# Copies of three weight sets move from GpSimd to SyncE, and the opening's steps get a new order

## The chip, the cores and the metric

The kernel runs on one NeuronCore of a Trainium2 chip. The core has five engines with an instruction stream each: TensorE (PE in the profile, with PEld for its weight loads), VectorE (DVE), ScalarE (ACT), GpSimd (POOL) and SyncE (SP), which here does nothing but issue DMAs. Sixteen DMA engines move the data. Each engine works through its own stream in program order; an instruction that waits holds everything behind it on that engine. The metric is the time of one execution on the device in microseconds.

## What is computed

The input x has 2048 rows of 576 floats. Its layer norm feeds two branches, and both are added to x:

```python
x = A_x
xn = _layernorm(x, axis=-1)
return x + _A_ref(xn, A_wqkv, A_wo) + _B_ref(xn, B_w1, B_w2)
```

Branch A is attention with 32 heads of 18 features. Each position looks at 8 keys, at distances 0, 2, ... 14 backwards; `wqkv` is 576 x 1728 and `wo` is 576 x 576. Branch B is `relu(xn @ w1) @ w2` with `w1` 576 x 4608 and `w2` 4608 x 576. All is float32, and the matrix products have to be that exact.

## The kernel before

**Precision and tiling.** Each float32 operand of a matmul is split into a high part (a copy to the matmul's float type, on ScalarE) and a low part (the rest, a subtraction on VectorE, in the opening sometimes on GpSimd), both by `hi_lo`. A product is then three matmuls: high by high, high by low and low by high. The rows of x are handled in two phases (`ph`) of 1024 rows, each in two halves (`h`) of 512, each in two blocks (`j`) of 256. The first products, of xn with `w1` and `wqkv`, use a Strassen-like scheme with seven products P1 to P7 in a step (`pstep`); a step covers one weight set and one half of the rows.

**Weight sets.** The columns of `w1` and `wqkv` are cut into sets of 256. A set of kind F is a piece of `w1` (with the matching rows of `w2`), one of kind Q a piece of `wqkv`. In phase 0 the order is F0, Q0, Q1, F1, Q2, F2, Q3 and so on; these are sets 0, 1, 2, 3, 4, 5, 6. Two buffers `wset` hold two sets at a time. For set s, `set_make` issues six loads on SyncE, from a copy of the set in DRAM that lies in the order in which it is read (`W1C`, `W2C`, `WQC`: w1c, w2c, wqc in the profile). One of the six goes to the tile `ts` and the others to slots of `wset`. VectorE then forms the Strassen combinations, and ScalarE and VectorE form the high and low parts.

**The copies.** They are made in the kernel itself by DMAs within DRAM. In the regular course each is cut into pieces by `w1_keep`, `w2_keep` and `wq_keep`, four row blocks with a DMA for each column segment. `kept_part` (lines 478 to 484) issues a piece on GpSimd's queue. Ahead of each piece it puts a one-element copy into the tile `spare` that reads the latest tile of hidden values, `LATEST[-1]`, so that the pieces are paced by the progress of the work. Sets from number 5 on get such pieces through the plan of the main loop. Sets 2, 3 and 4 get them in the opening, by the steps K2, K3 and K4 (`keep_set`, line 1251).

**The opening.** Sets 0 and 1 are read straight from the inputs and used without Strassen, in steps written out by hand in `OPEN`, line 34. The letters are:

- `T`i: block i of 128 normalised rows is transposed by PE and stored in parts; this also gives out the normalising of block i+2
- `F`hjf: 14 matmuls of set 0 (`classic`), for half h, block j and column group f; the result goes through relu into a hidden tile `hb`
- `Q`hjf: 14 matmuls of set 1; VectorE transposes the result into a staging buffer `stg` (`q_out`), and when both blocks j of a pair (h, f) are in, SyncE stores the buffer to DRAM (`qd`)
- `B` and `O`: hidden tiles times `w2`, summed into the banks `po`; O steps are six matmuls each and are named O, then half, block, column group, row half. After the last one of a bank ScalarE copies the sum away and seeds the bank anew.
- `S`h: the Strassen sums of the rows of half h. The raw rows of the last two blocks lie in the tile `ts` until S1 has read them.
- `K`s: the DRAM copy of set s
- `M`: `set_make(2)`, the loads and conversions of set 2

Then the main loop runs steps t = 4, 5, ... (two for each set). At the first product of t = 4 it calls `set_make(3)`, at t = 6 `set_make(4)`. Set 5's copies come at t = 5 and 6.

**What sets the order.** PE's instructions are given out in the order of the steps. A planner in the kernel (`Order`) keeps a modelled clock for each engine and gives out the operations of ScalarE and VectorE in between: of those that are ready by its model, the one with the earliest due time. `dve(fn, n, after, slack)` hands it an operation with a modelled duration of n/960 + 0.068 us; `send` does so for a DMA on SyncE and `keep` for one on GpSimd. The planner decides the order only. At run time each instruction waits for the data that it needs.

Of the kernel before, what the change touches and what calls it, by code (L numbers as in the profile page):

```python
# [16 lines left out]
P = 128  # L17
NPH = 2
NI = 8
TBN = 256  # L20
# [11 lines left out]
WARM = 38  # L32
PADS = (16, 16, 32, 32)
OPEN = """
B0 T2 B1 T3 Q000 F010 T4 Q011 O0100 F011 T5 Q010 O0101 S0 T6 F101
F100 O0111 T7 S1 Q001 K2 O0110 Q100 O1001 O1000 F110 O1011 F111 K3 O1010 M2
O1101 O1111 K4 Q110 Q101 O1100 O1110 Q111
""".split()

S2, S4, S3, S1 = range(4)  # L40
T1, B11, T2, B21, T3, B22, T4, RR = range(8)
# [21 lines left out]
class Order:  # L63
# [94 lines left out]
    def dve(self, fn, n, after, slack, lag=0.0):  # L158
        op = Op(DVE, n / 960.0 + 0.068, fn, after, self.now() + slack, lag)
        self.wait[DVE].append(op)  # L160
        return op
# [6 lines left out]
    def send(self, fn, kb, after=(), margin=0.0):  # L168

        after = [a for a in after if a is not None]  # L170
        self.force(after)
        start = max([self.clk[SP], self.now() - 0.5] + [a.end for a in after])
        fn()
        op = Op(SP, 0.45, None, (), 0.0)
        self.clk[SP] = start + 0.45
        rate, tail = (250.0, 2.2) if start < 16 else (185.0, 1.2)
        self.dma = max(self.dma, start + 0.3, 1.0) + kb / rate
        op.end = max(start + 2.1, self.dma + tail) + margin
        return op
# [28 lines left out]
def tile_body(ctx: ExitStack, tc: tile.TileContext, x, wqkv, wo, w1, w2, out):  # L208
    nc = tc.nc
    S, D = x.shape  # L210
    F = w1.shape[1]
# [22 lines left out]
    def wide(s):  # L234
        return QW[SETS[s][2]] if SETS[s][1] == "Q" else P
# [9 lines left out]
    SEGS = [[] for _ in range(NQ)]  # L245
    y = 0
    for part, u, c0, c1 in FEATS:
        while c0 < c1:
            q, off = y // (2 * P), y % (2 * P)
            cnt = min(c1 - c0, 2 * P - off)  # L250
# [26 lines left out]
    act, dve, send, pe = o_.act, o_.dve, o_.send, o_.pe  # L277
# [190 lines left out]
    W1C = [dram.tile([D, 2 * P], F32, name=f"w1c{n}") for n in range(NP)]  # L468
    W2C = [dram.tile([2 * P, D], F32, name=f"w2c{n}") for n in range(NP)]
    WQC = [dram.tile([D, 2 * QW[q]], F32, name=f"wqc{q}") for q in range(NQ)]  # L470
# [3 lines left out]
    kept = {}  # L474
# [132 lines left out]
    T6 = 6 * 0.1135  # L607
# [3 lines left out]
    def stub():  # L611
        return Op(SP, 0.0, None, (), 0.0)
# [28 lines left out]
    def q_out(t, j, f, src, after, slack):  # L641
        s, h = t // 2, t % 2
        ph, _, q = SETS[s]
        wd = wide(s)
        if (t, f) not in STGOF:
            b = STGN[0] % NST
            STGN[0] += 1
            STGOF[t, f] = b, [], [], STGFREE[b], stub()
            STGFREE[b] = [STGOF[t, f][4]]
            QOUT.setdefault((ph, q), []).append(STGOF[t, f][4])  # L650
        b, got, ops, before, done = STGOF[t, f]

        def turn():
            if not got:
                got.append(stp[b].tile([P, 2, TBN], F32, name=f"stg{b}"))
            nc.vector.transpose(got[0][0:wd, j], src[0:wd])

        op = dve(turn, TBN, [*after, *before], slack)
        ops.append(op)

        def out_():
            if len(ops) < 2 or any(z.end is None for z in ops):
                return
            z = got[0]
            for a in range(wd // 32):
                dst = QD[ph, q][4 * h : 4 * h + 4, :, f * wd + 32 * a : f * wd + 32 * (a + 1)]
                e = send(
                    lambda: nc.sync.dma_start(
                        dst.rearrange("i (b r) c -> r (i b) c", r=32),
                        z[32 * a : 32 * (a + 1)].rearrange("r j (z c) -> r (j z) c", c=32),  # L670
                    ), 80, ops,
                )
            done.end = e.end

        op.post = out_
        return [op]

    def evict(t, j, f, src, after, slack):
        s, h = t // 2, t % 2
        ph, kind, n = SETS[s]  # L680
        if kind == "F":
            return h_parts((2 * (ph * NP + n) + h, j, f), src, after, slack)
        return q_out(t, j, f, src, after, slack)
# [566 lines left out]

    def keep_set(s):
        ph, kind, n = SETS[s]
        for f in [w1_keep, w2_keep] if kind == "F" else [wq_keep]:
            for z in range(4):
                f(n, z)
    for z in range(8):
        at_f(7 + z // 4, 3 * (z % 4) + 2, wo_keep, z)
    for z in range(4):
# [224 lines left out]
    def opening(step):  # L1483
        kind, z = step[0], [int(c) for c in step[1:]]
        if kind == "B":
            o_both(*z)
        elif kind == "T":
            turn_one(*z)
        elif kind == "Q":
            classic(2 * SQ0 + z[0], z[1], z[2], next_bank())  # L1490
        elif kind == "F":
            classic(z[0], z[1], z[2], next_bank())
        elif kind == "O":
            o_step(*z)
        elif kind == "K":
            keep_set(*z)
        elif kind == "S":
            h = z[0]
            SX[h] = s_forms(h, 30 + 2 * h)
            if h:  # L1500
                ts_free[0] = SX[1]
                SNF[5], SNF[2] = list(SX[0]), list(SX[1])
                VDONE[:] = SX[0]
                OFREE[1] = list(SX[1])
        elif kind == "M":
            set_make(2, True)
            for f in range(2):
                if SF[1] == 2:
                    w2_make(1, f)
# [10 lines left out]
    for t in range(4, 2 * NS):  # L1520
        ph, kind, n = SETS[t // 2]
# [48 lines left out]
```

## Time and profile before

| What | us |
|---|---|
| median of 3 runs | 1121.61 |
| lowest and highest | 1120.93 and 1122.43 |
| the profiled execution's own time | 1122.29 |
| its span, first to last instruction | 1120.5 |
| mean granted clock of TensorE | 0.996 of full |

The page gives each engine's busy time as a share of the span. A line of a timeline has the start, the duration, the engine, the line and the operation; several instructions in a row of one kind are drawn together with their count. `SPq` is SyncE's queue of DMA issues. A duration there runs from the first issue of the row to the end of the last, with what SyncE waited between them. The chain of waits goes back from the last instruction to what released it, step by step.

### The profile page before, as it was taken

The numbers are of one execution on the slowest core, as the hardware profiler recorded it, in microseconds if no ns is written. First come the engines' busy times: TensorE is split into PE (matmuls) and PEld (weight loads), VectorE is DVE, ScalarE is ACT, GpSimd is POOL, SyncE is SP. The second block draws the span as 40 slices with busy tenths as digits, with TensorE's granted clock in tenths as the row PEclk, the third lists the DMA queues.
The fourth block names the chain that finished last, engine by engine and source line by source line (L and its number), as shares of the span: only waits on it lengthen the run. The fifth ranks groups of instructions, "written<-read, shape, count | busy, mean of one in ns | idle before, by whom it ended". The sixth has DMA issues, their size and how long they took to land.

```text
span 1120.5 us, 24120 instructions
## 1 busy us (share of the span) xinstructions
PE 1103.9 (99%) x9047; PEld 1100.9 (98%) x9047; DVE 910.5 (81%) x1749; ACT 757.3 (68%) x1561; POOL 247.6 (22%) x506
## 2 busy tenths in 40 slices
PE   9979999999999999999999999999999999999998
PEld 8979999999999999999999999999999999999998
DVE  7657999999998989954785698989998998997440
ACT  7646666666678677686794666667677776767774
POOL 4744365243443533700110000000000000000000
PEclk9989999999999999999999999999999999999999
DMA  5489487857655463363364844564625315224212
GB/s 153 94 189 240 118 210 181 192 148 200 180 152 160 122 185 91 85 173 94 92 192 83 193 99 89 135 130 86 149 91 119 105 47 140 75 55 86 79 48 86
DMA packets 326502, 144.16 MB, mean 129 GB/s; under 512 B 209648, under 2 KB 306608, under 8 KB 325104
## 3 DMA queue, kind: packets, MB, share of 16 engines
q1 hardware_dynamic: 315408, 113.40, 41.1%
q0 software_dynamic: 10816, 28.92, 9.2%
q8 instruction: 71, 1.16, 0.5%
q14 instruction: 47, 0.39, 0.1%
q10 hardware_dynamic: 160, 0.30, 0.1%
HBM read 118.42 MB, written 50.66 MB: 151 GB/s over the span
## 4 chain that ended last, share of the span: by engine, by line
PE 92%; DMA 2%; ACT 2%; POOL 2%; DVE 1%; issue 1%; SPq 0%; DVEq 0%; ACTq 0%; POOLq 0%
PE po L341 44%; PE bk L341 28%; PE pm L341 13%; PE bkA L341 8%; DMA wset<-w1c 1%; POOL wqc L482 1%; POOL spare L481 1%; DMA wset<-wqc 0%; DMA x<-in_x 0%; ACT wset L335 0%; DVE bst L376 0%; ACT xs L335 0%; ACT po L335 0%; SPq L528 0%; PE pm L411 0%
## 5 line engine op out<-in xcount | busy, mean ns | idle before, releaser
L341 PE MATMUL po<-w2t,hb 128*128 128x256 f32 (+1 forms) x3456 | 503.7, 292 | 1.1 <-ACT po L335 1.1
L341 PEld LDWEIGHTS po<-w2t,hb 128*128 128x128 f32 x3456 | 463.1, 187 | 1.6 <-ACT po L335 1.5
L335 ACT ACTIVATE x<-po 128x576 f32<-128x576 f32 x286 | 186.3, 652 | 227.9 <-PE po L341 227.3
L341 PE MATMUL bk<-xs,wset 128*128 128x256 f32 (+1 forms) x1584 | 224.3, 278 | 0.8 <-ACT sn L335 0.8
L341 PEld LDWEIGHTS bk<-xs,wset 128*128 128x128 f32 (+1 forms) x1584 | 202.8, 187 | 1.1 <-ACT sn L335 1.0
L335 ACT ACTIVATE po<-x 128x576 f32<-128x576 f32 x286 | 187.1, 654 | 6.1
L481 POOL COPY spare<-hb 1x1 f32<-1x1 f32 x228 | 106.9, 469 | 201.2 <-ACT hb L335 201.2
L341 PE MATMUL bk<-xa,wset 128*128 128x256 f32 (+1 forms) x888 | 125.7, 279 | 3.8 <-ACT wset L335 3.7
L341 PEld LDWEIGHTS bk<-xa,wset 128*128 128x128 f32 (+1 forms) x888 | 114.1, 188 | 4.3 <-ACT wset L335 3.8
L341 PE MATMUL pm<-xs,wset 128*128 128x256 f32 (+1 forms) x720 | 103.5, 280 | 3.7 <-ACT sn L335 3.2
L1113 POOL TENSOR_SCALAR_AFFINE_SELECT lg<-lg 1x512 f32<-1x512 f32 x8 | 9.6, 1206 | 416.8 <-DVE lg L1110 416.8
L338 DVE TENSOR_TENSOR sn<-bk,sn 128x256 f32<-128x256 f32 (+1 forms) x132 | 55.3, 420 | 52.0 <-ACT hb L335 25.2
L341 PEld LDWEIGHTS pm<-xs,wset 128*128 128x128 f32 (+1 forms) x720 | 93.2, 189 | 4.2 <-ACT sn L335 3.4
L1107 DVE TENSOR_TENSOR pr<-qo,kk 128x1152 f32<-128x1152 f32 x64 | 85.5, 1347 | 5.4 <-DMA qo<-qd 3.7
L341 PE MATMUL bkA<-xa,wset 128*128 128x256 f32 (+1 forms) x624 | 88.2, 278 | 0.5 <-ACT bkA L335 0.5
L1110 DVE TENSOR_REDUCE lg<-pr 128x64 f32<-128x1152 f32 x64 | 85.4, 1340 | 0.2
L1139 DVE TENSOR_TENSOR pr<-lg,v 128x1152 f32<-128x1152 f32 x64 | 85.4, 1351 | 0.2
L341 PEld LDWEIGHTS bkA<-xa,wset 128*128 128x128 f32 (+1 forms) x624 | 81.5, 187 | 0.7 <-ACT bkA L335 0.7
L335 ACT ACTIVATE hb<-sn 128x256 fp32r<-128x256 f32 x140 | 57.4, 414 | 35.7 <-DVE sn L338 34.3
L341 PE MATMUL bk<-xr,wset 128*128 128x256 f32 (+1 forms) x412 | 80.4, 276 | 0.0
L338 DVE TENSOR_TENSOR wset<-ts,wset 128x512 fp32r<-128x512 f32 (+2 forms) x98 | 65.2, 666 | 10.5 <-ACT wset L335 10.1
L1146 DVE TENSOR_TENSOR pr<-pr 128x288 f32<-128x288 f32 (+1 forms) x128 | 71.6, 600 | 0.0
(159 smaller groups left out, 1574.0 us busy)
## 6 DMA issues: line engine op xcount, KB each, us to landing
w2t<-w2c SPq DMA_DIRECT2D x70, 288.0 KB, 3.4
qd<-stg SPq DMA_DIRECT2D x216, 64.0 KB, 2.1
wset<-w1c SPq DMA_DIRECT2D x105, 128.0 KB, 2.9
w1c<-in_w POOLq DMA_DIRECT2D x72, 144.0 KB, 3.4
w2c<-in_w POOLq DMA_DIRECT2D x72, 144.0 KB, 3.3
out<-x SPq DMA_DIRECT2D x16, 288.0 KB, 2.1
ts<-w1c SPq DMA_DIRECT2D x35, 128.0 KB, 2.8
wset<-w1c SPq DMA_DIRECT2D x70, 64.0 KB, 2.3
```

What stands on the lines that cost most here:

```text
L335: nc.scalar.activation(o, i, func)
L338: nc.vector.tensor_tensor(o, a, b, op=op)
L341: nc.tensor.matmul(o, l, r, start=start, stop=stop, skip_group_check=True)
L481: nc.gpsimd.tensor_copy(spare[0:1], f32(LATEST[-1])[0:1, 0:1])
L482: nc.gpsimd.dma_start(dst, src)
L1107: nc.vector.tensor_tensor(pr[i], q, window(k, i), op=ALU.mult)
L1110: nc.vector.tensor_reduce(s["lg"][:, i], pr.pop(i).rearrange(heads, d=Dh), axis=AX.X, op=ALU.add)
L1113: nc.gpsimd.affine_select(out=z, in_=z, pattern=[[1, NI], [1, W], [0, HG]], compare_op=ALU.is_ge, fill=-1e9 / scale, base=1 - W, channel_m ...
L1139: nc.vector.tensor_tensor(pr[i].rearrange(heads, d=Dh), e, window(VV[u % 2], i).rearrange(heads, d=Dh), op=ALU.mult)
L1146: nc.vector.tensor_tensor(o, z[:, 0:n], z[:, n : 2 * n], op=ALU.add)
```

## The change

Three things change. `OPEN` gets a new order, with the same steps. K2 stands after the first Q step and not behind Q001, K3 comes right after Q001, and K4 follows M2. `keep_set` no longer calls the paced pieces of GpSimd: it issues whole copies on SyncE, one for each column segment of a Q set (four for set 2, three for set 4) and two for the F set 3, with no element copy ahead of them. The planned duration of the transpose in `q_out` grows by 25 elements, 26 ns in the planner's model.

```diff
 OPEN = """
-B0 T2 B1 T3 Q000 F010 T4 Q011 O0100 F011 T5 Q010 O0101 S0 T6 F101
-F100 O0111 T7 S1 Q001 K2 O0110 Q100 O1001 O1000 F110 O1011 F111 K3 O1010 M2
-O1101 O1111 K4 Q110 Q101 O1100 O1110 Q111
+B0 T2 B1 T3 Q000 K2 F010 F011 T4 Q011 O0101 T5 O0100 S0 O0110 T6
+Q001 K3 O0111 Q010 T7 F100 F101 F110 O1000 S1 O1001 O1010 F111 M2 K4 O1011
+Q111 Q100 Q110 O1100 O1101 O1111 Q101 O1110
 """.split()
...
-        op = dve(turn, TBN, [*after, *before], slack)
+        op = dve(turn, TBN + 25, [*after, *before], slack)
...
     def keep_set(s):
         ph, kind, n = SETS[s]
-        for f in [w1_keep, w2_keep] if kind == "F" else [wq_keep]:
-            for z in range(4):
-                f(n, z)
+        if kind == "Q":
+            for off, src, cnt in SEGS[n]:
+                kept.setdefault(("wq", n), []).append(
+                    send(lambda: nc.sync.dma_start(WQC[n][:, off : off + cnt], wqkv[:, src : src + cnt]), 2.6 * cnt)
+                )
+        else:
+            kept["w1", n] = [send(lambda: nc.sync.dma_start(W1C[n], w1[:, 2 * n * P : 2 * (n + 1) * P]), 650)]
+            kept["w2", n] = [send(lambda: nc.sync.dma_start(W2C[n], w2[2 * n * P : 2 * (n + 1) * P, :]), 600)]
```

`SEGS[n]` lists the column segments of the n-th Q set: its offset in the set, its offset in `wqkv` and its width. For Q1 (set 2) the widths are 16, 16, 144 and 80 columns, for Q2 (set 4) 64, 144 and 48.

## The prediction

> **What bounds the kernel now.** I read the page's busy table first, then PE's waits over the whole span, then windows, to see where those waits lie.
>
> ```profile
> PE 1103.9 (99%) x9047; PEld 1100.9 (98%) x9047; DVE 910.5 (81%) x1749; ACT 757.3 (68%) x1561; POOL 247.6 (22%) x506
> ```
> ```profile
> PE bk L341 <- ACT wset L335: 3.7, 1, 3.7
> PE pm L341 <- ACT sn L335: 3.2, 1, 3.2
> PE po L326 <- POOL mhalf L282: 1.3, 1, 1.3
> PE po L341 <- ACT po L335: 1.1, 2, 0.9
> ```
> ```profile
> 50.00:80.00 30.00, 23.19 (x177) 22.83 (x176) 14.40 (x36) 10.00 (x25) 16.46 (x50) 0.89 0.81 188
> 80.00:560.00 480.00, 480.00 (x3957) 480.00 (x3957) 414.83 (x788) 332.48 (x685) 194.17 (x384) 1.00 0.60 155
> 560.00:1000.00 440.00, 437.41 (x3613) 436.46 (x3612) 385.97 (x706) 299.96 (x618) 9.49 (x12) 1.00 0.47 112
> ```
>
> TensorE (PE) is busy 1103.9 of 1120.5 us, so only 16.6 us of idle time can be won without removing arithmetic. In the waits, each row names the waiting engine, tile and line, the releaser, the total, the count and the longest: two single waits, 3.7 and 3.2 us, are far ahead. The windows (length; then busy time and count of PE, its weight loads, VectorE, ScalarE, GpSimd; then granted clock, DMA share, GB/s) put the loss between 50 and 80 us, where PE was busy 23.19 of 30 us at a mean clock of 0.89. From 80 to 560 us PE never stops, and from 560 to 1000 it stops for 2.6 us. A time won before 80 us should therefore reach the end nearly in full.
>
> PE's timeline has the two holes (start, duration, instruction; in brackets the idle time before it):
>
> ```profile
> 46.06 2.50 PE L341 MATMUL po<-w2t,hb 128*128 128x256 f32 x18
> ...
> 58.55 1.62 PE L341 MATMUL bk<-xa,wset 128*128 128x256 f32 x6 [3.65 <-ACT wset L335]
> ...
> 61.55 0.85 PE L341 MATMUL bk<-xs,wset 128*128 128x256 f32 x6
> ...
> 63.14 0.84 PE L341 MATMUL bk<-xs,wset 128*128 128x256 f32 x6
> ...
> 72.12 1.65 PE L341 MATMUL pm<-xs,wset 128*128 128x256 f32 x6 [3.15 <-ACT sn L335]
> ...
> 75.17 0.86 PE L341 MATMUL pm<-xa,wset 128*128 128x256 f32 x6
> ```
>
> Each hole is dear twice. Fourteen matmuls of 256 columns, a product of six and one of eight, take 63.14 − 61.55 = 1.59 us at full clock. After the first hole the same fourteen take 61.55 − 58.55 = 3.00 us, 1.41 more; after the second 75.17 − 72.12 = 3.05 us, 1.46 more. The holes cost 3.65 + 1.41 + 3.15 + 1.46 = **9.67 us**.
>
> What made them is read from the chain of waits, then GpSimd's, SyncE's and VectorE's timelines:
>
> ```profile
> 52.12 4.80 DMA wset<-wqc
> ...
> 64.82 5.79 DMA wset<-w1c
> ```
> ```profile
> 48.50 0.53 POOL L482 DMA_DIRECT2D wqc<-in_wqkv  x1
> ```
> ```profile
> 11.23 2.05 SPq L1383 DMA_DIRECT2D x<-in_x  x4
> 31.51 9.87 SPq L668 DMA_DIRECT2D qd<-stg  x8
> 43.43 0.38 SPq L537 DMA_DIRECT2D wset<-wqc  x1
> 43.97 0.38 SPq L537 DMA_DIRECT2D ts<-wqc  x1
> 50.85 1.11 SPq L528 DMA_DIRECT2D wset<-wqc  x2
> 52.12 0.98 SPq L537 DMA_DIRECT2D wset<-wqc  x2
> 53.20 9.24 SPq L668 DMA_DIRECT2D qd<-stg  x8
> 62.61 0.39 SPq L537 DMA_DIRECT2D wset<-w1c  x1
> ```
> ```profile
> 43.23 1.29 DVE L338 TENSOR_TENSOR xs<-ts,xs 128x512 fp32r<-128x512 f32 x2
> ...
> 56.95 0.43 DVE L338 TENSOR_TENSOR ts<-wset,ts 128x256 f32<-128x256 f32 x1 [5.09 <-DMA wset<-wqc]
> ...
> 57.96 0.44 DVE L656 STREAM_TRANSPOSE stg<-bk 128x256 f32<-128x256 f32 x1
> ```
>
> The sixteenth and last piece of the copy wqc leaves GpSimd at 48.50 us. SyncE, loading set 2 out of that copy, issues two loads at 43.43 and 43.97, then stands until 50.85; its last two loads go out from 52.12 and land at 52.12 + 4.80 = 56.92. VectorE takes them up at 56.95, ScalarE converts, and PE goes on at 58.55. The second hole is the first one's echo. The stores at 53.20 keep SyncE for 9.24 us, because the transposes that feed them (one at 57.96) stood on VectorE behind the subtraction of 56.95. So set 3's loads start only at 62.61, the last lands at 64.82 + 5.79 = 70.61, and ScalarE, held by set 3's conversions, copies the tile sn for PE too late.
>
> **The change, part by part.**
>
> *36 pieces leave GpSimd.* K2, K3 and K4 were 16 + 8 + 12 pieces there. Was their issue the limit, or the DMA engines?
>
> ```profile
> 20.00:22.00 2.00, 2.00 (x19) 2.00 (x18) 1.90 (x7) 1.18 (x3) 0.39 (x1) 1.00 0.00 0
> 46.00:48.00 2.00, 2.00 (x17) 2.00 (x17) 1.00 (x2) 1.62 (x4) 2.00 (x7) 1.00 0.29 52
> 52.00:54.00 2.00, 2.00 (x19) 2.00 (x18) 0.00 (x0) 0.00 (x0) 2.00 (x7) 1.00 0.99 243
> 58.00:60.00 2.00, 1.45 (x7) 1.48 (x8) 2.00 (x7) 1.92 (x5) 1.80 (x6) 0.50 0.79 163
> ```
>
> At 46 to 48 us GpSimd is busy 2.00 of 2 us and the DMA engines are at 0.29: the issue. At 20 to 22 us the DMA engines are empty. The Trainium skill, "DMA: Bandwidth & Descriptors", section "Issuing engines are not separate DMA queues", speaks against the change: all issuers run on the same 16 engines, so another issuer saves only its sequencer's time. By the rule alone, had the engines been the limit, the gain would be 0; the 2.00 against 0.29 says that the sequencer's time was the limit here.
>
> *Nine DMAs join SyncE.* K2 stands after Q000 and K3 after Q001, both ahead of the first store, which isn't given out before the transposes of Q011 and Q001. They wait for nothing, so SyncE issues these six right behind the four x loads, at 11.23 + 2.05 = 13.28 us. No row shows SyncE issue a copy within DRAM. The lower bound is the 0.38 us of the load at 43.43, the upper one the 9.87 / 8 = 1.23 us of the stores at 31.51, waits included. Six end by 13.28 + 6 x 1.23 = 20.7 us, and SyncE's next work comes at 31.51: hidden. On the DMA engines they queue behind the x loads, which are through by 20. K2 and K3 are three matrices of 576 x 256 floats, 3 x 0.59 = 1.77 MB. At the 243 GB/s of 52 to 54 us, where copies and loads filled the engines (0.99), that is 7.3 us: done by 27. Narrow rows (16 columns, 64 bytes) may be slower; three times as slow would be 20 + 22 = 42 us, still before set 2 is loaded. I take 0 us, the nearer end, with bounds 0 and +1 (x tiles that land later). K4 goes behind set 2's loads; its three issues delay the stores behind them by 1.1 to 3.7 us, which four staging buffers cover. Without that cover, this is the price.
>
> *Set 2's loads.* They now wait only for their slots (read by F110 and F111) and for the tile ts, which S1 still reads. Before, PE ran from F111's end at 46.06 to 58.55 − 3.65 = 54.90 us: five O steps and three Q steps. Now there are five and four, and a Q step is fourteen matmuls, 1.59 us. F111 ends at 54.90 − 8.84 − 1.59 = 44.5 us, if the opening ends when it did. S1's subtractions at 43.23 freed ts for the load at 43.97. Now S1 is given out a few steps later but hurried by M2, and VectorE has the same work in all, so I take 44 to 47. Four loads from 50.85 on took 53.10 − 50.85 = 2.25 us to issue, so all six, from 44.5, are out by 48 us, or by 50 if ts comes at 47. The last landed 4.80 us after 52.12, and set 3's 5.79 after 64.82, both on crowded engines: between the issue itself, 48, and 50 + 5 = 55. I take 51. Conversion takes 58.55 − 56.92 = 1.6 us more: set 2 is ready at 52.6, within 49.6 to 56.6, against PE's 54.9. The first hole goes; up to 1.7 us may be left.
>
> *Set 3.* The transposes no longer stand behind set 2, the last stores leave near 55, set 3's loads follow some 7 us before the present 62.61 and land by 70.61 − 7 = 63.6. PE would come for sn at 72.12 − 3.15 − 1.41 − 3.65 = 63.9 us. The second hole goes; the bound left is 0.5 us.
>
> *What is late next.* GpSimd, rid of the three sets, comes to its pieces for set 5 soon after F111, and these fall on set 2's loads; that is why I took a crowded landing.
>
> *The new order of the opening.* The same matmuls run. The old wait before O1000 (the 0.9 in the 1.1 row) should go, as O0110 stands earlier. New ones may come: F011 right behind F010, O0101 before its bank is seeded, T6 nearer to T4, while VectorE is busy 1.90 of 2 us at 20 to 22. Nearest row: waits of up to 0.9 us on po. I take a net of 0, bounds −0.9 and +1.8 (two such waits).
>
> *TBN + 25.* It changes only a planned duration, by 26 ns, and so the order on ScalarE and VectorE in the rest. What it can touch is the 2.6 us that PE idles from 560 to 1000: net 0, bounds −1.5 and +1.5.
>
> **Sum.** 1122.29 − 9.67 = 1112.6 us against the profiled execution's own time (its span is 1120.5). That execution lies 0.7 us above the median of 1121.61, so I predict **1112.0 us**, 0.86% less. The clock rows bear on the ramp terms: it was 0.50 at 58 to 60 us. The Trainium skill, "TensorE: Matmul & The Clock Gate", section "What's actually happening", says that one idle window of about 3.4 us halves the clock until a busy window has passed. From that page's figures each ramp would lose an estimated 1.7 us and the holes 10.2; the trace agrees with the half clock, and its 1.41 and 1.46 stand.
>
> **Rivals.** (1) *Set 2 stays late* (0.11): S1 frees ts late or the loads crowd, and 2 to 4 us of the first hole with its ramp remain, with or without the echo: 1114.5 to 1119. For it: a margin of only 2.3 us. Against: SyncE's stand before 50.85 was for the copies alone. (2) *The new order stalls* (0.05): VectorE can't feed PE between 20 and 45 us, 2 to 5 us: 1114 to 1117. (3) *Slower* (0.04): the wait for ts takes the place of the wait for copies. It stands ahead of set 2's other loads, K4 and all stores in SyncE's queue. It decides if ts comes free after some 50 us, since the last loads then leave after the present 52.12; at 54 us both holes come 4 us later on one path: 1122 to 1128, say 1125. Against: ts was free by 43.97. (4) *It doesn't do what it says* (0.04): the copies can't run ahead and start with the stores at 31.51 us, on crowded DMA engines: 1120 to 1122.
>
> **Chances.** The forecast has 0.76, at 1109 to 1114.5. The range takes in the bounds of the unknown costs and most of rival 1: 1109 to 1117. A measurement of this kernel can tell 0.2%, 2.2 us, from no change: faster 0.91 (the forecast, and rivals 1 and 2 nearly whole), same 0.05, slower 0.04.
>
> **What would show it.** Right: nine DMAs on SyncE, six of them before 21 us; DMA engines busy between 20 and 27; no idle time over 1 us on PE between 50 and 80 and a clock of 1.00 there; set 3's loads at 55 to 57. Wrong: loads of set 2 issued after 50 us, a long stand of SyncE for ts, PE waiting for VectorE or ScalarE between 20 and 45 us, or new waits after 560 us.

## The result, and the profile after

| | kernel before | changed kernel |
|---|---|---|
| median, us | 1121.44 (6 runs, 1120.55 to 1122.43) | 1113.97 (6 runs, 1112.48 to 1115.05) |
| ratio to before, 95% interval | | 0.9933 (0.992 to 0.9946) |
| profiled execution: own time, span, us | 1122.29, 1120.5 | 1115.05, 1113.3 |

The change saves about 0.7%, 7.5 us. That is inside the range, on the side that was forecast, and 2 us short of the predicted 1112.0.

The busy table and windows of the changed kernel answer to those shown of before:

```profile
PE 1102.5 (99%) x9047; PEld 1098.6 (99%) x9047; DVE 909.0 (82%) x1749; ACT 756.2 (68%) x1561; POOL 218.3 (20%) x434
```
```profile
50.00:80.00 30.00, 30.00 (x252) 29.79 (x251) 18.78 (x47) 16.64 (x38) 8.72 (x26) 1.00 0.85 189
80.00:560.00 480.00, 477.61 (x3926) 477.15 (x3924) 414.68 (x786) 331.66 (x684) 184.89 (x361) 1.00 0.59 153
560.00:1000.00 440.00, 438.55 (x3625) 437.59 (x3624) 386.97 (x706) 298.02 (x615) 8.02 (x10) 1.00 0.47 112
```

From 50 to 80 us PE is busy 30.00 of 30 us at full clock, where it was 23.19 at 0.89: both holes are gone, with their slow restarts. But from 80 to 560 us, where it had never stopped, it now stops for 2.4 us. PE's waits over the whole span name them:

```profile
PE pm L341 <- DVE sn L338: 1.5, 1, 1.5
PE po L326 <- POOL mhalf L282: 1.3, 1, 1.3
PE bk L341 <- DVE sn L338: 0.9, 1, 0.9
PE bk L411 <- ACT pr L394: 0.6, 1, 0.6
PE bk L341 <- ACT sn L335: 0.6, 1, 0.6
```

The two rows that wait for VectorE's tile sn, 1.5 and 0.9 us, are waits that the kernel before did not have here. They stand 2 us apart in PE's timeline:

```profile
65.34 0.94 PE L341 MATMUL pm<-xa,wset 128*128 128x256 f32 x6
...
90.65 0.94 PE L341 MATMUL po<-w2t,hb 128*128 128x256 f32 x6
93.12 0.97 PE L341 MATMUL pm<-xa,wset 128*128 128x256 f32 x6 [1.53 <-DVE sn L338]
...
95.18 0.97 PE L341 MATMUL bk<-xa,wset 128*128 128x256 f32 x6 [0.85 <-DVE sn L338]
95.99 0.87 PE L341 MATMUL bk<-xs,wset 128*128 128x256 f32 x6
```
```profile
100.23 0.94 PE L341 MATMUL po<-w2t,hb 128*128 128x256 f32 x6
101.01 0.85 PE L341 MATMUL pm<-xa,wset 128*128 128x256 f32 x6
...
101.92 0.84 PE L341 MATMUL bk<-xa,wset 128*128 128x256 f32 x6
102.60 0.84 PE L341 MATMUL bk<-xs,wset 128*128 128x256 f32 x6
```

The first rows are of the changed kernel, the second of the kernel before, each pair the same product. (The first, at 65.34, is the one that stood at 75.17 before: 9.83 us ahead.) At 90.65 the changed kernel is 100.23 − 90.65 = 9.58 us ahead, nearly all of the predicted 9.67. At 95.99 it is 102.60 − 95.99 = 6.61 us ahead. So 3.0 us were given back within 5 us: 1.53 + 0.85 of waits, and the other 0.6 in matmuls around them, as 0.97 against 0.85 in the rows above. Later, 560 to 1000 us idles 1.45 us against 2.59 before, 1.1 us better. 6.6 + 1.1 = 7.7; the spans differ by 7.2. The last half a microsecond was not traced.

VectorE's timeline shows what sn stood behind, and SyncE's what that waited for:

```profile
85.28 0.42 DVE L628 SCALAR_TENSOR_TENSOR hb<-bk,hb 128x256 fp32r<-128x256 f32 x1 [1.47 <-ACT hb L335]
89.66 1.36 DVE L1107 TENSOR_TENSOR pr<-qo,kk 128x1152 f32<-128x1152 f32 x1 [3.96 <-DMA qo<-qd]
91.05 1.35 DVE L1110 TENSOR_REDUCE lg<-pr 128x64 f32<-128x1152 f32 x1
92.32 0.44 DVE L656 STREAM_TRANSPOSE stg<-bkA 128x256 f32<-128x256 f32 x1
92.69 0.38 DVE L338 TENSOR_TENSOR sn<-pm,sn 128x256 f32<-128x256 f32 x1
```
```profile
75.91 7.52 SPq L1061 DMA_DIRECT2D kk<-qd  x6
83.52 2.48 SPq L1061 DMA_DIRECT2D qo<-qd  x4
```
```profile
94.86 0.42 DVE L628 SCALAR_TENSOR_TENSOR hb<-bk,hb 128x256 fp32r<-128x256 f32 x1 [1.48 <-ACT hb L335]
95.92 1.36 DVE L1107 TENSOR_TENSOR pr<-qo,kk 128x1152 f32<-128x1152 f32 x1 [0.64 <-DMA qo<-qd]
```

The product at 89.66 is the first of the attention. It waits 3.96 us for the tile qo, which SyncE fetches from DRAM behind the six fetches of kk. Before, VectorE came to the same product at 95.28 and waited 0.64 us. It now comes 9.6 us earlier, and the data only 95.92 − 89.66 = 6.26 us earlier. The 3.3 us between the two came in three places. The fetch started 84.92 − 75.91 = 9.0 us earlier, which leaves 0.6. The six fetches of kk took 7.52 us to issue against 6.08 before, 1.4 more (SyncE's row of the kernel before follows). The last 1.3 came in the four fetches of qo, which landed 3.4 to 4.5 us after their issue against 3.0 to 3.5 before.

```profile
84.92 6.08 SPq L1061 DMA_DIRECT2D kk<-qd  x6
```

So qo comes later against the moment when it is wanted. The subtraction at 92.69, on which PE waits, is queued behind the attention's work.

### The profile page after: what moved, and what is told of

It reads as the page before. It is cut to its first block, busy times and chain, and to the rows that moved or that the text cites. A ratio compares the mean times of both kernels' runs of the same rounds, so it can differ in the third digit from the quotient of the medians.

```text
span 1113.3 us, 24046 instructions
## 1 busy us (share of the span) xinstructions
PE 1102.5 (99%) x9047; PEld 1098.6 (99%) x9047; DVE 909.0 (82%) x1749; ACT 756.2 (68%) x1561; POOL 218.3 (20%) x434
## 4 chain that ended last, share of the span: by engine, by line
PE 89%; DVE 3%; SPq 3%; DMA 2%; ACT 2%; issue 1%; POOL 0%; DVEq 0%; ACTq 0%
PE po L341 43%; PE bk L341 26%; PE pm L341 12%; PE bkA L341 7%; SPq L1061 1%; DMA qo<-qd 1%; DMA wset<-w1c 1%; DMA qo<-in_w 0%; DVE pr L1107 0%; DMA wqc<-in_wqkv 0%; DVE sn L338 0%; DVE stg L656 0%; DVE wset L338 0%; ACT x L335 0%; ACT hb L335 0%
## 5 line engine op out<-in xcount | busy, mean ns | idle before, releaser
L481 POOL COPY spare<-hb 1x1 f32<-1x1 f32 x192 | 94.6, 493 | 222.8 <-ACT hb L335 222.8
```

The source lines that it names most:

```text
L481: nc.gpsimd.tensor_copy(spare[0:1], f32(LATEST[-1])[0:1, 0:1])
```

## The experiments

The theory after the result had two halves. *First*, both holes came from the pace of GpSimd's pieces, so that any early copy removes them. *Second*, the loss at 93 us is VectorE standing in order behind the fetch of kk and qo, which came forward by less than PE because other transfers crowd it. Rivals: the new order did the work; the 26 ns moved the attention's product forward. All times are medians; the ratio is to the kernel before in the same group of runs (its medians were 1120.37 us beside e1 to e4, 1120.61 beside e5 to e8 and 1120.76 beside e9 to e12).

| run | edit | median us | ratio to before, 95% |
|---|---|---|---|
| e1 | before + copies on SyncE | 1116.05 | 0.9959 (0.9945 to 0.9973) |
| e2 | before + new order | 1125.48 | 1.004 (1.0025 to 1.0055) |
| e3 | changed, planned TBN | 1112.35 | 0.993 (0.9915 to 0.9945) |
| e4 | before + TBN + 25 | 1122.06 | 1.0013 (1.0002 to 1.0023) |
| e5 | e2 with K2 behind S0 | 1125.43 | 1.0037 (1.0022 to 1.0052) |
| e6 | before, K2 to K4 unpaced on GpSimd | 1113.31 | 0.9933 (0.992 to 0.9946) |
| e7 | changed, sets 5 and 6 unpaced | 1112.29 | 0.9926 (0.9912 to 0.994) |
| e8 | changed, fetches planned 4 us later | 1125.18 | 1.0044 (1.0025 to 1.0063) |
| e9 | changed kernel again | 1113.25 | 0.993 (0.9914 to 0.9946) |
| e10 | e7 with planned TBN | 1111.52 | 0.9918 (0.9903 to 0.9932) |
| e11 | e1 with K2, K3 behind Q000 | 1116.66 | 0.996 (0.9948 to 0.9973) |
| e12 | e6 + sets 5 and 6 unpaced | 1113.11 | 0.9931 (0.9917 to 0.9944) |

### The three parts by themselves (e1, e2, e4)

e1 puts only the new `keep_set` into the kernel before, e2 only the new `OPEN`, e4 only this line:

```diff
-        op = dve(turn, TBN, [*after, *before], slack)
+        op = dve(turn, TBN + 25, [*after, *before], slack)
```

> The kernel before with the new keep_set only: copies on SyncE, old order, no 25. Theory (the pace of GpSimd's pieces made both holes): the holes of 3.7 and 3.2 us with their slow restarts go, 1112 to 1115 us. Rival (the new order did it, by giving set 2's loads an earlier or freer place): the holes stay for the most part, 1118 to 1122 us.

e1 took 1116.05 us: more than the theory said, less than the rival. The copies alone bring 0.4%. Of the holes, waits of 0.17, 0.47 and 0.41 us were left near 55 to 58 us and one of 2.00 us at 70.42. In the old order K2 comes behind four stores in SyncE's queue and leaves only at 34.54 us, and K3 at 41.46: most of the early start is lost to the place in the queue.

> The new order with the copies still as paced pieces on GpSimd, no 25. K2 now stands ahead of the normalising of blocks 6 and 7 in GpSimd's queue: 16 pieces of 0.65 us or more. Theory: the copies are early enough for set 2, so the holes at 55 and 69 us go, but T6 waits 5 to 12 us for its scale behind the pieces, at some 29 us: 1117 to 1127 us. Rival (the order alone brings the gain, the issuer is indifferent): 1112 to 1115 us, no wait at T6.

e2 is slower than before, as the theory said. GpSimd's timeline of e2 shows the last piece of set 2 and then the two small operations of block 6's normalising, and ScalarE's what waits for these:

```profile
19.68 0.18 POOL L481 COPY spare<-hb 1x1 f32<-1x1 f32 x1
...
30.05 0.53 POOL L482 DMA_DIRECT2D wqc<-in_wqkv  x1
30.60 0.58 POOL L383 TENSOR_TENSOR rstd<-mv,mhalf 128x1 f32<-128x1 f32 x1
31.28 0.26 POOL L386 TENSOR_SCALAR nm<-mv,rstd 128x1 f32<-128x1 f32 x1
```
```profile
31.58 0.87 ACT L394 ACTIVATE pr<-x,nm,rstd 128x576 f32<-128x576 f32 x1 [9.94 <-POOL nm L386]
32.35 0.36 ACT L335 ACTIVATE hb<-bkA 128x256 fp32r<-128x256 f32 x1
```

Sixteen pieces hold GpSimd from 19.68 to 30.58. The scale of a normalising stands behind them, ScalarE stands 9.94 us for it, VectorE stands for ScalarE's part of a hidden tile, and PE 8.52 us for VectorE's part of it. The holes of before were gone (no wait of PE from 36 to 74 us); 8.5 us and the restart were paid instead. The wait wasn't at T6 but already at Q011, as ScalarE's evictions stood behind the normalising: the mechanism was foreseen, its victim not.

> The kernel before with TBN + 25 only. Theory: both holes stay, order shifts in the rest cost or bring up to 1.5 us: 1120 to 1123 us. Rival (the 25 elements have a share of the gain): below 1119 us.

e4 lies 0.13% above before, 0.02 to 0.23%: both holes stayed (2.8 and 2.6 us), and by themselves the 25 elements bring none of the gain.

### Is it SyncE, or the start and the pace? (e5, e6, e11)

e5 is e2 with K2 moved behind S0:

```diff
-B0 T2 B1 T3 Q000 K2 F010 F011 T4 Q011 O0101 T5 O0100 S0 O0110 T6
+B0 T2 B1 T3 Q000 F010 F011 T4 Q011 O0101 T5 O0100 S0 K2 O0110 T6
```

> The new order with paced pieces on GpSimd, but K2 put behind S0, where all normalising has been given out; no 25. Theory (set 2 needs its copy by some 45 us, whoever issues it): 16 pieces from 31 us on end at 42 to 46 us, no wait at T6, holes gone or below 1.5 us: 1113 to 1117 us. Rival (SyncE's issue itself is what helps): the holes stay, 1119 to 1122 us.

Both missed: 1125.43 us. I had taken it that all normalising was given out by S0. The planner gave out block 7's later, so its two operations again stood behind the pieces, from 26.64 to 37.91 us, and PE waited 6.36 us at T7. This run shows the price of the place once more, and nothing on the issuer.

e6 leaves the copies with GpSimd and the old order, and takes the pacing away for K2 to K4 (`free_run` is set for the pieces of `keep_set` alone):

```diff
-            nc.gpsimd.tensor_copy(spare[0:1], f32(LATEST[-1])[0:1, 0:1])
+            if not free_run:
+                nc.gpsimd.tensor_copy(spare[0:1], f32(LATEST[-1])[0:1, 0:1])
```

> The kernel before with the element copy ahead of each piece left out for K2, K3 and K4: same pieces on GpSimd, old order, no pacing. Theory (pace and start set the holes): pieces of 0.55 us from 29.5 us on, K2 through by 38, K3 by 43, K4 by 49 us; holes gone, 1112 to 1115 us. Rival (GpSimd can't issue fast enough in any case): at least 3 us of the first hole stay, 1117 to 1121 us.

e6 took 1113.31 us, ratio 0.9933, as much as the whole change. GpSimd's timeline of e6, then its window:

```profile
29.87 8.69 POOL L486 DMA_DIRECT2D wqc<-in_wqkv  x16
38.56 2.12 POOL L486 DMA_DIRECT2D w1c<-in_w  x4
40.67 1.95 POOL L486 DMA_DIRECT2D w2c<-in_w  x4
```
```profile
50.00:80.00 30.00, 30.00 (x254) 29.86 (x253) 18.85 (x47) 16.25 (x38) 11.60 (x35) 1.00 0.84 183
```

Sixteen pieces now take 8.69 us, 0.54 each, and are through at 38.56, ten us earlier than before. PE is busy 30.00 of 30 us. In the kernel before the first element copy had waited for a hidden tile until 34.67 us, where e6 starts at 29.87: that is 4.8 of the ten us. The other 5.7 are the element copies, 0.17 to 0.73 us each of GpSimd's time. Neither SyncE nor the new order is needed to remove the holes: start and pace are.

e11 is e1 with K2 and K3 right behind Q000 and K4 behind M2, the computing steps in the old order.

> The kernel before with copies on SyncE as in e1, but K2 and K3 right behind Q000 and K4 behind M2, so that the copies run as early as in the changed kernel while all computing steps keep their old order. Theory (what e1 lacked was the place of the copies in SyncE's queue): 1113 to 1115 us, no wait over 0.6 us from 50 to 75 us. Rival (the new order of the computing steps is needed): 1115.5 to 1117, waits as in e1 (2.0 us at 70, 1.1 us at 55 to 58).

The rival's time came, 1116.66 us, but not its waits. Near 55 us there are none; PE waits 1.00 us at O1000, 0.75 at 64.77 and 2.42 us at 91.85, the last with a slow restart, and there VectorE stands 4.50 us for qo:

```profile
84.72 0.42 DVE L628 SCALAR_TENSOR_TENSOR hb<-sn,hb 128x256 fp32r<-128x256 f32 x1
89.63 1.36 DVE L1107 TENSOR_TENSOR pr<-qo,kk 128x1152 f32<-128x1152 f32 x1 [4.50 <-DMA qo<-qd]
```

So the early place removed what e1 had left of the first hole, and the loss went to the next bottleneck. e11 and e6 have the same order of computing steps and early copies, and their medians lie 3 us apart; in the profiled executions e11 has that loss, and e6 waits 0.19 us there. Why the fetch of kk took 7.39 us to issue in e11 and 6.14 in e6 stays open.

### The loss at 93 us (e3, e7, e8, e9, e10)

e3 is the changed kernel without the 25 elements; e7 is the changed kernel in which the element copy is left out for sets 5 and 6:

```diff
-            nc.gpsimd.tensor_copy(spare[0:1], f32(LATEST[-1])[0:1, 0:1])
+            if key not in (("w1", 2), ("w2", 2), ("wq", 3)):
+                nc.gpsimd.tensor_copy(spare[0:1], f32(LATEST[-1])[0:1, 0:1])
```

> The changed kernel with the planned transpose at TBN again. Theory (the new waits of 1.5 and 0.9 us on VectorE at 93 us come from the fetch of qo, which lands late, and not from the planner's 26 ns): they stay, time within 2 us of 1114. Rival (the 25 elements placed the first product of the attention too early): the waits at 93 us go and the time falls to 1111 to 1112.

> The changed kernel with the element copies of sets 5 and 6 left out, so that GpSimd issues them from 50 us on and not at 70 to 81. Theory (those pieces crowd the fetch of kk and qo at 76 to 86 us and so make the waits at 93): the fetch lands 1.5 us earlier or more, the waits of 2.4 us shrink to below 1, 1111.5 to 1113. Rival (the fetch is bound by SyncE's issue and the stores ahead of it): the waits stay within 0.5 us, 1113.5 to 1115.

In e3 one of the two waits stayed, 0.82 us, and in e7 both went. SyncE's and VectorE's rows of e3, e7 and of both edits together (e10), in this order:

```profile
75.45 6.90 SPq L1061 DMA_DIRECT2D kk<-qd  x6
```
```profile
87.48 1.36 DVE L1107 TENSOR_TENSOR pr<-qo,kk 128x1152 f32<-128x1152 f32 x1 [2.13 <-DMA qo<-qd]
```
```profile
76.37 5.64 SPq L1062 DMA_DIRECT2D kk<-qd  x6
```
```profile
86.56 1.36 DVE L1108 TENSOR_TENSOR pr<-qo,kk 128x1152 f32<-128x1152 f32 x1 [0.78 <-DMA qo<-qd]
```
```profile
75.19 5.26 SPq L1062 DMA_DIRECT2D kk<-qd  x6
```
```profile
85.51 1.35 DVE L1108 TENSOR_TENSOR pr<-qo,kk 128x1152 f32<-128x1152 f32 x1
```

> The changed kernel itself, beside the others of this group. 1113 to 1115 us.

> The changed kernel with the element copies of sets 5 and 6 left out and the planned transpose at TBN. Theory (the waits at 93 us have two separate helps, the free fetch and VectorE's order): no wait over 0.5 us from 60 to 110 us, at least as fast as with the free fetch alone, 1111 to 1112.5 us. Rival (the two help the same wait, or the reordering costs elsewhere): no gain over either, 1112.5 to 1114.

e9 is the changed kernel again, and its median of 1113.25 us is inside what was expected. The table sets these runs beside e6, e11 and e12 (below). Its third column is the share of the DMA engines' time that GpSimd's queue took while the kk fetches were issued.

| | K2 to K4 issued by | GpSimd's share | six kk fetches issued in, us | VectorE's wait for qo | PE's waits at 93 us | median us |
|---|---|---|---|---|---|---|
| before | GpSimd | 25% | 6.08 | 0.64 | none | 1121.44 |
| changed; again (e9) | SyncE | 28%; 28% | 7.52; 7.58 | 3.96; 3.69 | 1.53 + 0.85; 1.27 + 0.85 | 1113.97; 1113.25 |
| e3 | SyncE | 29% | 6.90 | 2.13 | 0.82 | 1112.35 |
| e7 | SyncE | 0 | 5.64 | 0.78 | none | 1112.29 |
| e10 | SyncE | 0 | 5.26 | none | none | 1111.52 |
| e11 | SyncE | 26% | 7.39 | 4.50 | 2.42 | 1116.66 |
| e6 | GpSimd | 25% | 6.14 | 1.47 | 0.19 | 1113.31 |
| e12 | GpSimd | 0 | 6.17 | 0.34 | none | 1113.11 |

From the changed kernel over e3 to e7 and e10, a shorter fetch goes with shorter waits of VectorE and PE. In e7 GpSimd's twenty pieces of sets 5 and 6 leave from 30.75 to 41.55 us, where the changed kernel's DMA engines have room at first (share 0.05, 0.00 and 0.11 from 30 to 36 us); in the changed kernel twelve of them leave from 73.07 to 81.48, across the fetch. So with SyncE's copies, taking the pieces away shortens the fetch, as the theory said. But the pieces by themselves can't be what made the fetch longer than before. In the kernel before the same twelve leave from 82.62 to 91.05, across a fetch of 6.08 us and with nearly the same share of the DMA engines: they are paced by the work and moved forward with it, by 9.55 us. And e6, which has the pieces across the fetch, and e12, which has none there, issue it in the same time (e6, then e12):

```profile
77.14 6.14 SPq L1065 DMA_DIRECT2D kk<-qd  x6
```
```profile
76.95 6.17 SPq L1065 DMA_DIRECT2D kk<-qd  x6
```

With the pieces of sets 5 and 6 paced, the fetch took 6.90 to 7.58 us in all six runs with K2 to K4 on SyncE (changed, e1, e3, e8, e9, e11) and 6.05 to 6.86 us in all five with them on GpSimd (before, e2, e4, e5, e6). Why, no run shows, and so the cause of the longer fetch stays open. That VectorE stands for qo, and PE behind VectorE, is shown.

The rival on the 25 elements holds in part, as e3's wait for qo is shorter too; in the medians, the intervals of e3 and e7 overlap that of the changed kernel, so a gain from either edit alone isn't shown. e10 has the lowest median, 1111.52, and no wait of PE over 0.5 us from 60 to 110 us; its interval overlaps those of e7 and e9, so its 1.7 us against e9 are likely and not certain.

e8 tried the other cure: the planner is told that the first unit's fetches land 4 us later.

```diff
             if got:
-                got.end = z.end
+                got.end = z.end + (4.0 if o_.now() < 150 else 0.0)
```

> The changed kernel with the planner told that the first unit's fetches land 4 us later (a planned figure only; no data moves otherwise). Theory (VectorE stands in order behind a product whose qo has not landed, with PE's subtractions behind it): the product comes later in VectorE's order, the waits of 1.5 and 0.9 us at 93 us go, 1111 to 1112.5. Rival (PE there waits for set 7's loads or conversions anyway): a wait of 1.5 us or more for another releaser at 92 to 98 us, 1113 to 1115.

Both missed widely: 1125.18 us. The waits of VectorE at 93 us went (PE has one of 1.35 left at 98.70), but the attention's work, given out later, was still late at the end of the first phase. PE's timeline of e8 near the end of the first phase:

```profile
483.18 1.65 PE L341 MATMUL pm<-xs,wset 128*128 128x256 f32 x6 [4.02 <-ACT sn L335]
...
493.13 0.95 PE L341 MATMUL pm<-xa,wset 128*128 128x256 f32 x6 [0.74 <-DVE sn L338]
...
499.01 0.97 PE L341 MATMUL bk<-xs,wset 128*128 128x256 f32 x6 [1.13 <-ACT bkA L335]
```

There the products and transposes of an attention unit fill VectorE from 469 to 484 us, and a weight set's subtractions come between them only from 479.10 on. ScalarE stands 7.18 us for these, copies sn for PE behind their conversion, and PE stops for 4.02 us with a slow restart. From 440 to 500 us PE is busy 53.98 of 60 us at a mean clock of 0.94; the changed kernel is busy 60.00 at 1.00. Most of the 11 us that e8 costs against the changed kernel lie there.

### The pieces without pacing in the old order (e12)

> The kernel before with the element copies left out for K2, K3, K4 and for sets 5 and 6; everything stays on GpSimd, in the old order, without 25. Theory (pacing was the whole fault, for the later sets as well): no wait over 0.5 us from 50 to 110 us, 1111.5 to 1113. Rival (GpSimd's pieces of sets 5 and 6, now behind K4's at 49 to 62 us, crowd set 3's loads at 58): a wait of 1 us or more at 62 to 75 us, 1113.5 to 1116.

e12 took 1113.11 us, just above the theory's range and below the rival's: from 80 us on no wait of PE until 560, but 1.67 us at 65.65, the wait that the rival had named. Twenty more pieces on GpSimd leave behind K4's and fall on set 3's loads; VectorE stands 1.97 us for one of these, 0.89 us in e6. At 93 us there was little left to win, as e6 waits only 0.19 us there. Against e6 no difference can be told.

## Why the prediction was right, and where it fell short

- **Pieces bound by their issue.** Right in the main: e6 removes the holes with the same pieces on the same engine by issuing them earlier and faster. But a good part of what the prediction put down to the sequencer's time was the pacing: the first element copy's wait and the element copies themselves. The Trainium skill, "DMA: Bandwidth & Descriptors", section "Issuing engines are not separate DMA queues", says that who issues is indifferent to the DMA engines. No run tests that by itself: e6 and the changed kernel have the same ratio, 0.9933, but not the same order, and e11, with SyncE's copies in e6's order, is 3 us slower. The section adds that the time to start a DMA is usually small beside the DMA. The trace agrees for one piece: in e6 it took 0.54 us to start and some 3.0 us to land. Sixteen in a row held GpSimd for 8.69 us even so.
- **Nine DMAs on SyncE.** Right: six leave from 13.89 to 20.05 us (20.7 was the bound), and the DMA engines are empty at 24 us (share 0.92 at 22 to 24, 0.00 at 24 to 26), 3 us before the estimate. Two of the six took 2.18 and 1.32 us to issue, more than the bound of 1.23 for one, and the six together stayed hidden. K4's three took 1.87 us, within the forecast.
- **Set 2.** Right: F111 ends at 44.34 us, where PE's next step begins (forecast 44.5), the load of ts leaves at 45.00 (44 to 47), the last load is out at 48.32, and P1 starts without a wait at 54.59, where the hole had begun at 54.90. SyncE stood 4.4 us for S1's tile xs ahead of that load of ts. A long stand there had been named as a sign of being wrong; this one did no harm. The cover was thinner than forecast: the copy on ScalarE for which PE had waited before (it ended at 58.50, the fifth into wset) now ends at 53.44, 1.15 us ahead of PE and not 2.3.
- **Set 3.** Right: its loads start at 57.32 (55 to 57 was forecast) and PE doesn't stop. In e9, the same kernel, 0.73 us of wait is left there, a little over the bound of 0.5.
- **New order.** Within its bounds: the 0.9 us at O1000 is gone, and 0.51 at 30.47 came, a wait for VectorE between 20 and 45 us, which had been named as a sign of being wrong. (0.43 us at 10.21 isn't the order's: e9, the same kernel, doesn't have it, and e1, in the old order, has 0.49.) What the order is worth depends on who copies: with paced pieces on GpSimd it costs 0.4% (e2), with SyncE's early copies it brings 4 us (e3 against e11, 1112.35 and 1116.66).
- **25 elements.** Within the bounds: alone +0.13%.
- **"A time won before 80 us should therefore reach the end nearly in full".** This step failed. It rested on the row in which PE never stops from 80 to 560 us, but that row says nothing of how little slack the other engines have: 0.64 us of wait at 95.92 on VectorE was a sign that the fetch of qo landed just in time. Of the 9.58 us that were won, 3.0 were lost there, 1.1 came back after 560 us, and between the two profiled executions the term stands at 7.2, not 9.67. The bounds of the forecast covered this, though they had been drawn for other terms: that part is luck.
- **The size of the holes.** Part of the shortfall may lie in the 9.67 us itself. It was read from an execution of 1122.29 us, at the slow end of this kernel's runs (1118.18 to 1123.11 in the later groups). e6, which waits only 0.19 us at 93 us, saves 9.1 us between the profiled executions (spans 1120.5 and 1111.4) but 7.3 us between the medians (1120.61 and 1113.31). No trace shows the holes of a median execution.
- **What is late next.** I named GpSimd's pieces for set 5, and they came where I said (from 45.54 us) without harm. What was late next was qo at 93 us, which no rival had named.

## What to carry to other kernels

When a stall is removed, the work behind it comes forward, but not all by the same amount: here a product came 9.6 us earlier, the start of its fetch 9.0 and its data 6.3. Look through the next stretch for waits that are small but not zero, on any engine, since each of them may be a chain with no slack. A queue is a place in an order before it is an engine: the same small copies are harmless, or cost 8 us when the two short operations of a normalising stand behind them. And before moving work to another engine, try it on the same engine without the brake: here that alone gave the same 0.7%.

## What the runs showed of the hardware

The time to issue a DMA on SyncE isn't a constant: six fetches of the same shapes took 5.26 us (e10) to 7.58 us (e9), without a wait that the profile shows. How busy the DMA engines were doesn't settle it: their share during the fetch was 1.08 in the kernel before (6.08 us), 1.05 in the changed kernel (7.52) and 0.83 in e12 (6.17).

The clock's drop isn't settled by the length of the waits. The changed kernel and e9 are the same program; each stops twice at 93 us, for 1.53 + 0.85 and 1.27 + 0.85 us, and e9's windows show a clock that fell:

```profile
90.00:100.00 10.00, 7.61 (x61) 7.16 (x60) 9.63 (x18) 4.77 (x11) 0.15 (x1) 1.00 0.87 252
```
```profile
90.00:100.00 10.00, 7.87 (x52) 7.45 (x51) 8.80 (x16) 3.82 (x8) 1.67 (x2) 0.83 0.89 266
```

The first is the changed kernel (clock 1.00), the second e9 (0.83), with the shorter waits. Six matmuls on bk, the product after the second wait, took 1.65 us in e9 (at 95.36) where they took 0.97 in the other (at 95.18). The Trainium skill, "TensorE: Matmul & The Clock Gate", section "What's actually happening", has the clock decided by a free-running window of 3.4 us; that the same waits cost the clock in one execution and not in the other agrees with a window that isn't bound to the program, though here no single wait filled one. The section asks for an idle window before the clock falls; here it fell after waits of 1.27 and 0.85 us, and in e11 after a single one of 2.42 us (0.50 at 92 to 94 us), so the measurement decides. A clock of 0.83 over 10 us is what (1 − 0.83) × 10 / 0.5 = 3.4 us at half clock (0.50 at 96 to 98 us) would give, an estimate that fits one such window. It costs an estimated (1 − 0.83) × 10 = 1.7 us, so it can be a part of why e9's runs lie 5 us apart (1111.91 to 1116.98, the profiled execution); the others left no trace.
